# Row maxima kept in six neighbouring columns and transposed once for both heads, with a re-planned order of the work

## The chip, the cores and the metric

The kernel runs as one launch on one core of a Trainium2 chip. The metric is the device time of an execution in microseconds (us). TensorE (PE in the rows) does the matrix products and transpositions, VectorE (DVE) and ScalarE (ACT) read their results out of PSUM, GpSimd (POOL) works from SBUF alone, and SyncE (SP) issues the transfers.

## The reference

Two layers of attention follow each other, for 4 batches of 768 positions, in float32. The first has 8 heads of 64 dimensions; a query attends only to the keys that fall in its own cluster (the nearest of 16 centroids). The second is a mixture of four experts with a causal mask, of which each position uses two:

```python
mask = q_assign[:, :, :, None] == k_assign[:, :, None, :]
scores = scale * np.matmul(q, k.transpose(0, 1, 3, 2))
scores = np.where(mask, scores, -1000000000.0)
scores = scores - np.max(scores, axis=-1, keepdims=True)
attn = np.exp(scores)
attn = attn / (np.sum(attn, axis=-1, keepdims=True) + 1e-09)
...
for e in range(E):
    ...
    scores = np.where(causal, -1000000000.0, scores)
    scores = scores - scores.max(-1, keepdims=True)
    ...
    out += mask[..., None] * w[:, :, kk:kk + 1] * ye
```

What matters here is the row's maximum, which is subtracted before the exponential.

## The kernel before

The work is cut into 24 pairs (`NS`): 16 pairs of heads of the first layer (`n` from 0 to 15), then 8 pairs of experts. A pair holds two heads or experts `h`, and its 768 queries are done in two halves `hf` of 384, each of three chunks `cc` of 128. So there are 48 halves.

For each half, `core(n)` does the same steps:

- **Row matmuls** (L1084): one product per chunk, head and half of the keys gives scores with queries on the partitions, in a PSUM bank of the tag `row` (two banks). VectorE takes the maximum along each row (L1094) into `mx`, and L1099 joins the two key halves into `MT`, a tile of 128 x 2 x 2 x 128 in which chunk `cc` of head `h` and half `hf` has its column at 32 `cc`. The other columns are zero.
- **Transposition of the maxima** (L1106): two TensorE transpositions, one per head, of 128 x 128 from `MT` into one bank of the tag `misc`. The three rows that are wanted come out at partitions 0, 32 and 64.
- **Copy and transfer**: for every pair but the first, ScalarE (L1116) or VectorE (L1119) copies 96 partitions x 256 columns, negated, to `mr`, and two transfers put every 32nd row of `mr` into row `MR` of the query tile `tq`. For the first pair, where the rows start at partitions of 32 each, ScalarE writes them straight into `tq` (L1131, six small copies a half).
- **Scores** (L1158, L1159): two accumulating products per key chunk and head, with keys on the partitions, in a bank of the tag `st` (three banks). The second holds the row `MR`, so that the maximum is subtracted by the product. ScalarE takes the exponential (L1164) into `p` tiles.
- **Values and sums**: products with the values (L1202, two heads beside each other in the array, into the one bank `av`), additions of the `p` tiles on GpSimd (L479) or VectorE (L480), and their sums over keys (L1226).

Before that, `attention_operands(n)` transposes queries and keys (L626), finds each position's cluster, and multiplies the queries by the mask of one half of the clusters: a product of the cluster rows with a block matrix (L766), read by VectorE (L770 for the first pair alone, L776, L782) and ScalarE (`hi`). For the first pair these two products take the banks `row`. In that pair ScalarE also copies cluster rows into `tq` (L734). `moe_operands` does the like for experts with projections (L870, L922). While the first pair waits for its inputs, TensorE runs products with no use (L1330).

The order of the work is written out: each step is an `op` with a number in the order in which it was created, and the table `ORDER` gives for each engine the list of its numbers. `Plan.run` follows that table; each engine executes its list strictly in that order, and a step that may run on two engines runs on the one in whose list it stands. The banks and tiles of a tag are handed out in turn to their users.

Of the kernel before, what the change touches and what calls it, by code (L numbers as in the profile page):

```python
# [10 lines left out]
def _warn_once_fixed(msg, *args, **kwargs):  # L11
# [26 lines left out]
    pe="""  # L38
# [373 lines left out]
def t_mm(n):  # L412

    return max(n / 2400 + 0.015, 0.111)
# [8 lines left out]
def kernel(  # L423
# [133 lines left out]
    for s in range(3):  # L557
        TK.append(consts.tile([128, 2, 2, S], FR, name=f"tk{s}"))
        TQ.append(consts.tile([128, 2, 2, S], FR, name=f"tq{s}"))
    MT = consts.tile([128, 2, 2, 128], FT)  # L560

    def clear_rows(s):
        for h in range(2):
# [821 lines left out]
```

## Time and profile before

| | us |
|---|---|
| median of 3 runs | 722.25 (720.97 to 724.99) |
| profiled execution | 721.82 |
| its span, first to last instruction | 720.1 |
| TensorE busy | 702.6 (98%) |
| VectorE busy | 567.5 (79%) |
| ScalarE busy | 365.8 (51%) |
| GpSimd busy | 303.1 (42%) |

The span is 1.7 us shorter than the time of the same execution; what lies around it is start and end of the launch. "Busy" counts an engine as busy from the start of an instruction to its end. TensorE's matmuls overlap, so two starts that lie 0.18 us apart show as instructions of 0.34 us each: the distance from start to start says what one costs in a stream, not its own duration. In a timeline row, "x2" joins two instructions that follow each other, the second number is the time from the first one's start to the last one's end, and a bracket gives the idle time before it and what ended it.

### The profile page before, as it was taken

The numbers are of one execution on the slowest core, as the hardware profiler recorded it, in microseconds if no ns is written. First come the engines' busy times: TensorE is split into PE (matmuls) and PEld (weight loads), VectorE is DVE, ScalarE is ACT, GpSimd is POOL, SyncE is SP. The second block draws the span as 40 slices with busy tenths as digits, with TensorE's granted clock in tenths as the row PEclk, the third lists the DMA queues.
The fourth block names the chain that finished last, engine by engine and source line by source line (L and its number), as shares of the span: only waits on it lengthen the run. The fifth ranks groups of instructions, "written<-read, shape, count | busy, mean of one in ns | idle before, by whom it ended". The sixth has DMA issues, their size and how long they took to land.

```text
span 720.1 us, 13669 instructions
## 1 busy us (share of the span) xinstructions
PE 702.6 (98%) x4609; PEld 529.2 (73%) x4609; DVE 567.5 (79%) x1279; ACT 365.8 (51%) x904; POOL 303.1 (42%) x245
## 2 busy tenths in 40 slices
PE   6999999999999999999999999999999999999997
PEld 4666767677667677667677688868977987887776
DVE  6989887988888878888889876785598678578844
ACT  4365656556456465456466643464355345333642
POOL 5043467437357575554775632242222223112220
PEclk9999999999999999999999999999999999999999
DMA  7696664685676667595686564445455444455223
GB/s 193 170 195 170 157 173 112 164 221 131 155 201 166 185 166 176 133 232 151 169 213 187 145 175 120 118 126 145 145 130 143 125 123 139 104 125 149 76 77 124
DMA packets 79794, 109.99 MB, mean 153 GB/s; under 512 B 23936, under 2 KB 63212, under 8 KB 79724
## 3 DMA queue, kind: packets, MB, share of 16 engines
q1 hardware_dynamic: 79724, 109.11, 58.5%
q8 instruction: 37, 0.61, 0.4%
q14 instruction: 33, 0.27, 0.1%
HBM read 36.54 MB, written 12.91 MB: 69 GB/s over the span
## 4 chain that ended last, share of the span: by engine, by line
PE 81%; DMA 7%; DVE 4%; SPq 3%; ACT 3%; issue 1%; ACTq 0%; DVEq 0%
PE av L1202 20%; PE row L1084 11%; PE st L1158 11%; PE st L1159 10%; PE misc L870 9%; PE misc L922 5%; PE misc L1315 4%; SPq L467 3%; PE misc L1226 3%; PE misc L626 2%; DVE mx L1094 2%; DMA tq<-hi 2%; PE misc L650 1%; PE misc L1106 1%; DMA tk<-hi 1%
## 5 line engine op out<-in xcount | busy, mean ns | idle before, releaser
L1094 DVE TENSOR_REDUCE mx<-row 128x1 f32<-128x384 f32 (+1 forms) x442 | 232.0, 547 | 49.2 <-PE row L1084 46.0
L1158 PE MATMUL st<-tq,tk 128*128 128x384 f32 (+2 forms) x528 | 182.5, 348 | 2.5 <-ACT p L1164 1.8
L1164 ACT ACTIVATE p<-st 128x384 f32<-128x384 f32 (+2 forms) x304 | 128.5, 459 | 100.4 <-PE st L1159 61.8
L1159 PE MATMUL st<-tq,tk 97*128 97x384 f32 (+2 forms) x528 | 174.0, 332 | 0.4 <-DMA tq<-mr 0.4
L1084 PE MATMUL row<-tk,tq 80*128 80x384 f32 (+3 forms) x506 | 170.0, 359 | 1.7 <-DMA tq<-hi 1.3
L1084 PEld LDWEIGHTS row<-tk,tq 80*128 80x128 f32 (+1 forms) x506 | 92.9, 189 | 28.6 <-DVE mx L1094 9.7
L1158 PEld LDWEIGHTS st<-tq,tk 128*128 128x128 f32 x528 | 100.0, 189 | 16.6 <-issue 6.7
L1159 PEld LDWEIGHTS st<-tq,tk 97*128 97x128 f32 x528 | 100.4, 190 | 1.7 <-DMA tq<-mr 0.7
L479 POOL TENSOR_TENSOR acc<-acc,p 128x768 f32<-128x768 f32 (+2 forms) x39 | 64.8, 1660 | 74.5 <-DVE acc L480 38.0
L479 POOL TENSOR_TENSOR acc<-acc,xl 128x768 f32<-128x768 f32 x29 | 53.2, 1833 | 31.6 <-DVE acc L480 29.0
L474 ACT ACTIVATE hi<-misc 128x384 fp32r<-128x384 f32 x72 | 35.3, 498 | 58.8 <-PE misc L870 37.8
L1164 ACT ACTIVATE xl<-st 128x384 f32<-128x384 f32 x112 | 51.9, 497 | 23.4 <-PE st L1159 22.9
L1164 ACT ACTIVATE xh<-st 128x384 f32<-128x384 f32 x112 | 52.4, 499 | 19.5 <-PE st L1159 18.9
L1169 POOL TENSOR_SCALAR_AFFINE_SELECT p<-p 128x256 f32<-128x256 f32 x48 | 21.3, 457 | 95.6 <-ACT p L1164 70.0
L1202 PE MATMUL av<-p,vt 128*64 128x384 f32 x320 | 59.4, 494 | 0.0
L479 POOL TENSOR_TENSOR acc<-p,p 128x768 f32<-128x768 f32 (+1 forms) x14 | 24.6, 1756 | 72.5 <-ACT p L1164 42.1
L479 POOL TENSOR_TENSOR acc<-acc,xh 128x768 f32<-128x768 f32 x24 | 44.0, 1831 | 22.0 <-DVE acc L480 19.4
L480 DVE TENSOR_TENSOR acc<-acc,p 128x768 f32<-128x768 f32 (+2 forms) x52 | 45.8, 880 | 5.4 <-POOL p L1169 1.7
L1092 DVE TENSOR_TENSOR row<-row,tri 128x128 f32<-128x128 f32 x96 | 28.1, 293 | 19.6 <-PE row L1084 19.4
L1277 POOL TENSOR_TENSOR xt<-avu,rb 128x384 f32<-128x384 f32 x28 | 28.2, 1021 | 35.3 <-DMA rb<-rd 31.3
L1202 PE MATMUL av<-p,vm 128*64 128x384 f32 (+2 forms) x288 | 41.5, 423 | 0.0
L1202 PE MATMUL av<-xl,vt 128*64 128x384 f32 x224 | 40.2, 491 | 0.0
(255 smaller groups left out, 1295.8 us busy)
## 6 DMA issues: line engine op xcount, KB each, us to landing
tq<-hi SPq DMA_DIRECT2D x91, 192.0 KB
tk<-hi SPq DMA_DIRECT2D x60, 192.0 KB
tk<-lo SPq DMA_DIRECT2D x46, 192.0 KB
tq<-lo SPq DMA_DIRECT2D x46, 192.0 KB
rb<-rd SPq DMA_DIRECT2D x46, 192.0 KB
vt<-in_v_dram SPq DMA_DIRECT2D x16, 384.0 KB
x<-xt SPq DMA_DIRECT2D x16, 384.0 KB
tk<-hi SPq DMA_DIRECT2D x16, 384.0 KB
```

What stands on the lines that cost most here:

```text
L474: return op("act", t_act(n, sbuf), lambda: ACT.activation(dst(), src(), AF.Copy), due, after, use, alt=(MO["m_copy"], "dve", t_dve(n), lam ...
L479: ways = [("pool", t_pool(n), lambda: POOL.tensor_tensor(dst(), a(), b(), op=fn)), ("dve", t_dve(n), lambda: DVE.tensor_tensor(dst(), a(), ...
L480: ("dve", t_dve(n), lambda: DVE.tensor_tensor(dst(), a(), b(), op=fn))]
L870: PE.matmul(m()[:, :HW], w_[:, dc, es], x_[dc]()[:, c], start=(i == 0), stop=(i == 3 * DC - 1))
L922: PE.matmul(m()[:, :NV], x_[dc]()[:, ts], w_[:, dc, :], start=(i == 0), stop=(i == 3 * DC - 1))
L1084: PE.matmul(ps()[:, :w], Q[0:R, h, 0, c * 128:(c + 1) * 128], K[0:R, h, 0, i * w:(i + 1) * w], start=True, stop=True)
L1094: DVE.tensor_reduce(to, ps()[:, :w], axis=AX.X, op=OP.max)
L1158: PE.matmul(p()[:, o_:HW], K[:, h, 1, ks], Q[:, h, 1, qs], start=True, stop=False)
L1159: PE.matmul(p()[:, o_:HW], K[0:R, h, 0, ks], Q[0:R, h, 0, qs], start=False, stop=True)
L1164: ACT.activation(pt()[:, h, o_:HW], p()[:, o_:HW], AF.Exp, scale=SC)
L1202: PE.matmul(av()[h * 64:(h + 1) * 64, o_:HW], d["vv"](h, kc), pt()[:, h, o_:HW], start=(kc == 0), stop=(kc == nk - 1), tile_position=(0, 6 ...
L1315: PE.matmul(m(), a_()[:, ts], w_()[:, ep, :], start=(ep == 0 and i == 0), stop=(ep == EP - 1 and i == 2))
```

## The change

1. The maxima of all pairs but the first go into a new tile `M6` of 128 x 2 x 2 x 3: the six columns of a half (two heads, three chunks) lie beside each other. The first pair keeps `MT`.
2. For these pairs one transposition of 128 x 6 gives 6 rows of 128, where two of 128 x 128 gave 128 rows of 256.
3. `mr` shrinks from 96 x 2 x 128 to 6 x 128, and so does its copy; the two transfers read three neighbouring partitions each.
4. The first pair's two mask products (L766) take banks of `st` in place of `row`.
5. The table `ORDER` is another one throughout. 133 steps change between ScalarE and VectorE (69 to VectorE, 64 away), 77 between GpSimd and VectorE (43 to VectorE, 34 away).

```diff
@@ ORDER (a line of each of the five lists; all five are new)
-8 4 15 0 13 1 185 18 189 194 20 196 199 361 23 25 42 201 37 50 58 52 204 68 54 56 70 62 60 206 64 66 72 78 219 80 82
+8 4 15 0 13 1 185 18 189 194 20 196 199 361 23 25 37 42 201 52 50 54 68 66 58 204 64 206 70 60 62 56 78 72 219 82 80
...
+    M6 = consts.tile([128, 2, 2, HC], FT)
...
-            m = misc() if n else plan.buf(psum, "row", (128, 512), FT, 2)
+            m = misc() if n else plan.buf(psum, "st", (128, 512), FT, 3)
...
+            def tops(h, n=n, hf=hf):
+                return M6[:, hf, h] if n else MT[:, hf, h, :32 * HC:32]
...
-                    to = mx()[:, h, cc, i:i + 1] if nb == 2 else MT[:, hf, h, 32 * cc:32 * cc + 1]
+                    to = mx()[:, h, cc, i:i + 1] if nb == 2 else tops(h)[:, cc:cc + 1]
...
-                for h in range(2):
-                    PE.transpose(m()[:, h * 128:(h + 1) * 128], MT[:, hf, h], identf)
+                if n:
+                    PE.transpose(m()[:2 * HC, :128], M6[:, hf].rearrange("p h c -> p (h c)"), identf)
+                else:
+                    for h in range(2):
+                        PE.transpose(m()[:, h * 128:(h + 1) * 128], MT[:, hf, h], identf)
...
-                mr = tmp("mr", (96, 2, 128), FR, bufs=2)
+                mr = tmp("mr", (2 * HC, 128), FR, bufs=2)
...
-                    ACT.activation(mr(), m()[:96, :256].rearrange("p (h j) -> p h j", h=2), AF.Copy, scale=-1.0)
+                    ACT.activation(mr(), m()[:2 * HC, :128], AF.Copy, scale=-1.0)
...
-                        dma(Q[MR:MR + 1, h, 0, hf * HW:(hf + 1) * HW], mr()[0:96:32, h])
+                        dma(Q[MR:MR + 1, h, 0, hf * HW:(hf + 1) * HW], mr()[h * HC:(h + 1) * HC])
```

Three places show how the order moves. The line numbers of the changed kernel are 4 to 7 higher from `core` on (L1088 is the row matmul that was L1084, L1110 the transposition, L1165 and L1166 the scores, L1209 the values, L1233 the sums) and 1 lower in the helpers (L473 and L474 are the copies).

TensorE, pair 7, at the transposition for its second half, which the trace has at 226.0 us; before:

```order
L1226 MATMUL misc_3128<-acc_2816,ones_82 32x192 x4
L1158 MATMUL st_3135<-tq_106,tk_105 128x384
L1159 MATMUL st_3135<-tq_106,tk_105 128x384
L1106 MATMUL misc_3143<-identf,MT 128x128 x2
L1158 MATMUL st_3146<-tq_106,tk_105 128x384
L1159 MATMUL st_3146<-tq_106,tk_105 128x384
L1084 MATMUL row_3151<-tk_107,tq_108 128x384
```

and now:

```order
L1233 MATMUL misc_3120<-acc_2794,ones_82 32x192 x4
L1110 MATMUL misc_3128<-identf,M_110 6x128
L1165 MATMUL st_3130<-tq_106,tk_105 128x384
L1166 MATMUL st_3130<-tq_106,tk_105 128x384
L1088 MATMUL row_3137<-tk_107,tq_108 128x384
L1088 MATMUL row_3140<-tk_107,tq_108 128x384
```

Two transpositions of 128 columns became one of 6, and it moved ahead of one pair of score products, to directly behind the sums.

ScalarE, first pair, from the cluster rows on; before:

```order
L706 ACTIVATE rows_303<-misc_299,row_bias,row_scale 128x384
L474 ACTIVATE hi_335<-row_323 128x384
L474 ACTIVATE hi_335<-row_317 128x384
L734 ACTIVATE tq_104<-rows_303 16x384 x2
L474 ACTIVATE hi_442<-misc_271 128x384
```

and now:

```order
L706 ACTIVATE rows_301<-misc_297,row_bias,row_scale 128x384
L734 ACTIVATE tq_104<-rows_301 16x384 x2
L473 ACTIVATE xk_325<-misc_268 128x384
L473 ACTIVATE hi_344<-st_319 128x384
L473 ACTIVATE hi_344<-st_317 128x384
```

The copies of the cluster rows into `tq` now stand ahead of the masked queries' high parts, and a copy `xk` of the second pair's keys stands between them.

VectorE, first pair, up to the joined maxima of its second half; before:

```order
L1094 TENSOR_REDUCE mx_470<-row_551 128x1
L475 COPY xq_573<-misc_553 128x384
L1094 TENSOR_REDUCE mx_470<-row_579 128x1
L639 TENSOR_TENSOR lo_518<-misc_567,hi_442 128x384
L475 COPY xq_573<-misc_581 128x384
L1094 TENSOR_REDUCE mx_470<-row_599 128x1
L1094 TENSOR_REDUCE mx_470<-row_565 128x1
L1099 TENSOR_REDUCE MT<-mx_470 128x2x3
```

and now:

```order
L1098 TENSOR_REDUCE mx_462<-row_569 128x1
L474 COPY xk_325<-misc_583 128x384
L1098 TENSOR_REDUCE mx_462<-row_590 128x1
L1098 TENSOR_REDUCE mx_462<-row_588 128x1
L1104 TENSOR_REDUCE MT<-mx_462 128x2x3
L639 TENSOR_TENSOR lo_518<-misc_583,hi_480 128x384
```

One of the copies and the subtraction `lo` no longer stand ahead of the joined maxima.

## Rows read from the trace of the kernel before

**Rows 1.** The page's first part: busy us (share of the span) xinstructions.

```profile
PE 702.6 (98%) x4609; PEld 529.2 (73%) x4609; DVE 567.5 (79%) x1279; ACT 365.8 (51%) x904; POOL 303.1 (42%) x245
```

**Rows 2.** Middle stretch: length, busy PE PEld DVE ACT POOL, PEclk, DMA share, GB/s.

```profile
40.00:680.00 640.00, 633.70 (x4163) 478.38 (x4160) 516.59 (x1157) 333.33 (x832) 283.98 (x212) 1.00 0.60 154
```

**Rows 3.** TensorE's timeline around a transposition of 24 columns (start us, us).

```profile
474.71 0.34 PE L1158 MATMUL st<-tq,tk 128*128 128x384 f32 x1
474.88 0.34 PE L1159 MATMUL st<-tq,tk 97*128 97x384 f32 x1
475.06 0.34 PE L1158 MATMUL st<-tq,tk 128*128 128x384 f32 x1
...
475.81 0.33 PE L1159 MATMUL st<-tq,tk 97*128 97x384 f32 x1
475.98 0.27 PE L966 MATMUL misc<-identf,wt 128*24 128x128 f32 x1
476.01 0.42 PE L1084 MATMUL row<-tk,tq 80*128 80x384 f32 x1
476.27 0.34 PE L1158 MATMUL st<-tq,tk 128*128 128x384 f32 x1
```

**Rows 4.** TensorE's timeline around one of the pairs of transpositions.

```profile
225.81 0.34 PE L1159 MATMUL st<-tq,tk 97*128 97x384 f32 x1
225.99 0.38 PE L1106 MATMUL misc<-identf,MT 128*128 128x128 f32 x2
226.13 0.42 PE L1158 MATMUL st<-tq,tk 128*128 128x384 f32 x1
226.39 0.34 PE L1159 MATMUL st<-tq,tk 97*128 97x384 f32 x1
```

**Rows 5.** All transpositions of L1106 and L966: ns min/median/max, first and last start.

```profile
L1106 PEld LDWEIGHTS misc<-identf,MT x96: 137/142/146, 32.3 to 683.1; 128*128 128x128 f32 x96
L1106 PE MATMUL misc<-identf,MT x96: 270/272/332, 32.3 to 683.2; 128*128 128x128 f32 x96
...
L966 PEld LDWEIGHTS misc<-identf,wt x4: 92/93/93, 475.8 to 650.2; 128*24 128x24 f32 x4
```

**Rows 6.** Waits of TensorE's matmuls: us in total, times, longest.

```profile
PE st L1158 <- ACT p L1164: 1.8, 5, 0.6
PE row L1084 <- DMA tq<-hi: 1.3, 3, 0.5
PE misc L1106 <- DVE MT L1099: 1.0, 3, 0.6
...
PE st L1158 <- ACT xh L1164: 0.6, 2, 0.4
PE st L1159 <- DMA tq<-mr: 0.4, 1, 0.4
```

**Rows 7.** Of the waits of TensorE's weight loads, the one for the row banks.

```profile
PEld row L1084 <- DVE mx L1094: 9.7, 22, 0.6
```

**Rows 8.** Copies of the transposed maxima, and a narrower copy, by form: busy, mean ns.

```profile
L1116 ACT ACTIVATE mr<-misc 96x256 fp32r<-96x256 f32 x34 | 12.9, 378 | 27.7 <-PE misc L1106 27.6
L1164 ACT ACTIVATE p<-st 128x128 f32<-128x128 f32 x32 | 8.4, 278 | 5.9 <-PE st L1159 5.8
L1119 DVE TENSOR_SCALAR mr<-misc 96x256 fp32r<-96x256 f32 x12 | 5.0, 414 | 2.5 <-PE misc L1106 2.5
```

**Rows 9.** VectorE's timeline in the first pair, up to its second joined maxima.

```profile
38.30 0.56 DVE L1094 TENSOR_REDUCE mx<-row 128x1 f32<-128x384 f32 x1 [0.90 <-PE row L1084]
39.35 0.56 DVE L639 TENSOR_TENSOR lo<-misc,hi 128x384 fp32r<-128x384 f32 x1 [0.50 <-ACT hi L474]
39.83 0.55 DVE L475 COPY xq<-misc 128x384 f32<-128x384 f32 x1
...
41.34 0.17 DVE L1099 TENSOR_REDUCE MT<-mx 128x6 f32<-128x12 f32 x1
```

More of the change, by code (lines that the diff above doesn't have):

```diff
@@ L1087, in core, with go @@
                 o = op("pe", t_mm(w), go, due, d["half_row"] if early and i == 0 else d["need_row"][hf], used)
-                def go(hf=hf, h=h, cc=cc, i=i, nb=nb, w=w, ps=ps, mx=mx):
+                def go(h=h, cc=cc, i=i, nb=nb, w=w, ps=ps, mx=mx, tops=tops):
                     if moe and i == nb - 1:
@@ L1097, in core, with go @@
             if two:
-                def go(hf=hf, mx=mx, two=two):
-                    DVE.tensor_reduce(MT[:, hf, :, 32 * two[0]:128:32][:, :, :len(two)], mx()[:, :, two[0]:], axis=AX.X,
-                                      op=OP.max)
+                def go(n=n, hf=hf, mx=mx, two=two):
+                    to = M6[:, hf, :, two[0]:] if n else MT[:, hf, :, :32 * HC:32]
+                    DVE.tensor_reduce(to, mx()[:, :, two[0]:], axis=AX.X, op=OP.max)
                 maxes.append(op("dve", 0.13, go, due + 0.6, maxes + last, [mx]))
             m = misc()
-            def go(hf=hf, m=m):
-                for h in range(2):
-                    PE.transpose(m()[:, h * 128:(h + 1) * 128], MT[:, hf, h], identf)
+            def go(n=n, hf=hf, m=m):
+                if n:
[3 more added lines that the diff above has]
+                        PE.transpose(m()[:, h * 128:(h + 1) * 128], MT[:, hf, h], identf)
             due = t_r + DUE["top"] + 6 * DUE["row_step"] * hf
-            o = op("pe", 2 * t_mm(128), go, due, maxes, [m])
+            o = op("pe", t_mm(128) if n else 2 * t_mm(128), go, due, maxes, [m])
             d["m_pe"].append(o)
@@ L1111, in core @@
             if n:
-                mr = tmp("mr", (96, 2, 128), FR, bufs=2)
+                mr = tmp("mr", (2 * HC, 128), FR, bufs=2)
                 def go_a(m=m, mr=mr):
-                    ACT.activation(mr(), m()[:96, :256].rearrange("p (h j) -> p h j", h=2), AF.Copy, scale=-1.0)
+                    ACT.activation(mr(), m()[:2 * HC, :128], AF.Copy, scale=-1.0)
                 def go_d(m=m, mr=mr):
-                    DVE.tensor_scalar(mr(), m()[:96, :256].rearrange("p (h j) -> p h j", h=2), -1.0, None, op0=OP.mult)
-                o = op("act", t_act(256), go_a, due + 0.4, [o], [m, mr], alt=(MO["m_copy"], "dve", t_dve(256), go_d))
+                    DVE.tensor_scalar(mr(), m()[:2 * HC, :128], -1.0, None, op0=OP.mult)
+                o = op("act", t_act(128), go_a, due + 0.4, [o], [m, mr], alt=(MO["m_copy"], "dve", t_dve(128), go_d))
                 def go(hf=hf, mr=mr):
                     for h in range(2):
-                        dma(Q[MR:MR + 1, h, 0, hf * HW:(hf + 1) * HW], mr()[0:96:32, h])
+                        dma(Q[MR:MR + 1, h, 0, hf * HW:(hf + 1) * HW], mr()[h * HC:(h + 1) * HC])
                 outs.append(op("sp", 2 * [(0.78, 0.05)], go, due + 0.5, [o] + sets_free(n), [mr]))
```

331 rows, old and new, of tables (act, dve, pe, pool) are left out of this document.

## The prediction

> **What bounds the kernel now.** I read three views in turn. The page's first part gives TensorE 98% busy, VectorE 79%, ScalarE 51%, GpSimd 42% [rows 1]. A busy share alone does not say that an engine sets the time, so the second view is the busy time of the middle, from 40 to 680 us: TensorE is idle there for 640 - 633.70 = 6.3 us in all, at the full granted clock (1.00, the level of 2.4 GHz) [rows 2]. The third is the timeline, since TensorE's instructions overlap: three score products of 384 columns start at 474.71, 474.88 and 475.06, 0.175 us apart while each shows 0.34 us [rows 3]. So TensorE issues products back to back, each held up only by the one ahead of it. What it no longer has to issue in the middle comes off the end, unless a wait swallows it.
>
> The Trainium skill speaks against the first of these readings (Trainium Kernel Development and Optimization, Performance Expectations): matmul busy time is a poor measure because matmuls are pipelined, and the share of the weight loads is a better one. By that, 529.2 us or 73% [rows 1] leaves a quarter of the span open. The trace agrees that the busy share overstates the work, and settles it by the spacing of the starts, which leaves no gap in the rows shown. The forecast goes by the spacing.
>
> **The change part by part.**
>
> Transpositions. There are 96 of L1106 [rows 5]; 4 are the first pair's and stay, so 92 in 46 steps become 46. What a pair costs in the stream: from the L1159 at 225.81 to the L1159 at 226.39 lie 0.58 us, in which TensorE starts a product, the two transpositions and another product [rows 4]. Two products without anything between take 475.06 - 474.71 = 0.35 us [rows 3], so the pair costs 0.23. What a single narrow one costs is in the trace too: L966 transposes 24 columns to 24 rows. From the L1159 ahead of it at 475.81 to the L1158 behind the next product at 476.27 lie 0.46 us; less 0.35 that is 0.11 [rows 3]. The difference is 0.12 by these rounded starts; half of the pair is 0.115, and I take 0.115. 46 x 0.115 = 5.3 us less on TensorE.
>
> The load of 24 columns shows 93 ns against 142 for 128 [rows 5], yet its transposition costs in the stream what half a pair costs. A rule of the Trainium skill would give more (TensorE: Matmul & The Clock Gate, LDWEIGHTS): a weight load takes its columns divided by 1.2 GHz, so 6 columns load some 100 ns sooner than 128. If that set the transposition's place in the stream, the sum would be lower by an estimated 46 x 0.10 = 4.6 us. The trace does not bear it out, neither in the load's duration nor in its cost; it stands among the rivals with a price from rows.
>
> Copies of the maxima. 34 on ScalarE at 378 ns and 12 on VectorE at 414 [rows 8] read 128 columns in place of 256. A ScalarE row with 128 columns has 278 ns, so I take 0.10 us less each, 4.6 us over both engines. It lies beside TensorE's work: ScalarE is busy for 51%. It also brings `tq` forward by 0.1 us per half, but only one wait of TensorE was for that transfer, 0.4 us [rows 6]. I count nothing; the bounds are 0 and -0.4.
>
> Transfers. The same two per half, with the same bytes into `tq`; only the source's partitions lie closer. Nothing.
>
> Joined maxima in `M6`. The same reductions with the same inputs, written to neighbouring columns in place of columns 32 apart. No row shows whether that pitch costs a write anything. VectorE's instruction at the joined maxima of the first pair is 0.17 us long with the wide pitch [rows 9], which bounds a gain by 46 x 0.17 on an engine with slack; a loss has no reason, since the new columns are contiguous. Nothing.
>
> First pair. ScalarE's copies into `tq` move ahead of the high parts, and the row products find their two banks free of the mask products, so these products can start earlier. But until the first joined maxima VectorE has the same list of instructions to do in the old and the new order, and it is the engine that is busy there. Only behind that does something move: a subtraction and a copy no longer stand ahead of the second joined maxima. The subtraction took 0.56 us, behind 0.50 of waiting for ScalarE [rows 9]; the copy's place is taken by another one. So the second joined maxima may come up to 1.1 us sooner, and TensorE, which by then also has the second pair's operands to work on, gains between nothing and that: I take -0.4. On the other side, the first row products that use `st` banks must now wait for a subtraction L782 on VectorE; the nearest row is VectorE's wait of 0.90 for a row product there [rows 9], so the other bound is +0.9.
>
> The new order elsewhere. TensorE's list moves its steps by two places on average and holds the same work. In the place shown the transposition comes two products sooner after the maxima, 0.35 us less time for VectorE to finish; elsewhere it comes later. 14 steps more end up on VectorE, at some 0.5 to 0.95 us each about 10 us on an engine that is idle for 150. I cost the order at nothing on balance, and this is the largest unknown: the prices are in the rivals.
>
> What waits swallow. Where TensorE waits for something that does not move with it, the time saved since the last such wait is lost. In the middle it waited 3 + 3 + 5 + 2 + 1 = 14 times for VectorE, ScalarE or a transfer, for 5.1 us [rows 6]. Most releasers (exponentials of scores, maxima of row products) themselves follow TensorE's work and come earlier with it; the transfers do so less. Half of 14 waits, each swallowing one step's 0.115, is 0.8 us. The bounds are 0 and all 14, 1.6 us.
>
> The sum, made against the profiled execution: 721.82 - 5.3 - 0.4 + 0.8 = 716.9 us. That execution lies 0.43 under the median of the runs, so I predict 717.3 us. What a measurement of this kernel can tell from no change is about 0.5%, or 3.6 us; faster means below 718.6, slower above 725.9.
>
> **The rivals.**
>
> The new order waits more for the row banks (slower). The place is the row product, L1084, whose weights wait for VectorE's maximum of the product two before it: 9.7 us in 22 waits, 0.44 each, in the old order [rows 7]. They lie inside TensorE's busy time, so its 98% would hide more of them. VectorE gets 14 steps more, and each that stands between two maxima can add such a wait. To end over 725.9 the order must add 725.9 - 717.3 = 8.6 us, 20 waits, nearly twice what there was; at 24 more the time is 728. For it: all five lists are new, and VectorE has the most work after TensorE. Against it: VectorE is idle for a fifth of the span [rows 1], and over 48 halves only 22 such waits stood. Chance 0.12.
>
> The saving is swallowed (no change). The 0.115 us of a step is small beside the waits, and if the transfers' chain rather than TensorE sets the pace of a pair, what TensorE saves it waits for later. It decides from 718.6 - 717.3 = 1.3 us on, three more waits of 0.44 at the row banks; with half of the 5.3 us gone the time is 720 us. For it: VectorE must finish a pair's maxima, 24 of them, and its other work within each pair. Against it: 6.3 us of idle time in 640 [rows 2]. It is also how the change would fail to do what it says. Chance 0.22.
>
> The narrow weight load shortens the remaining transposition as well. If what is loaded sets the transposition's place in the stream, one of 6 columns costs next to nothing in place of 0.11, and the sum falls by up to 46 x 0.11 = 5.1 us more, to 712.2. For it: the load of 24 columns is shorter than that of 128 [rows 5]. Against it: the one of 24 columns in the rows still cost the full 0.11 [rows 3]. This is the page's rule on weight loads taken to its end. Chance 0.06.
>
> **How the numbers follow.** The forecast, TensorE bound and the saving passed on, has 0.60, with its own range from 715.0 (no wait swallows anything, the first pair gains 0.9 and the order gives 1) to 719.5 (all 14 waits swallow and the order costs 1.4). About 0.06 of it lies above 718.6. Faster: 0.54 + 0.06 from the weight load + 0.03 of the swallowed case = 0.63. Slower: 0.12. Within 0.5%: 0.25. The range that should hold the time 8 times in 10 goes from 713.0, which leaves out the fullest gain of the narrow load, to 724.0, which takes in the swallowed case and a worse order up to 15 more waits at the row banks, and leaves out the slower one.
>
> **What would show it.** Right: the spacing around the single transposition is 0.46 for two products and it, as with L966; 50 transpositions of L1110 and L1113 in place of 96; TensorE's idle time in the middle still near 6 us; the waits of row products for maxima still near 10 us. First pair: the second joined maxima some 0.4 us earlier than 41.34. Wrong: the transposition costs 0.2 us although it is one; or the waits of L1088's weights for maxima go well above 22; or the middle's idle time rises by as much as the transpositions saved, at the transfers of `tq` and `tk`.

## The result, and the profile after

| | before | changed |
|---|---|---|
| median of the runs (us) | 722.95 (720.97 to 724.99) | 714.91 (714.00 to 716.05) |
| profiled execution (us) | 721.82 | 715.09 |
| its span (us) | 720.1 | 713.4 |
| granted clock of TensorE | 0.999 | 0.999 |

The ratio is 0.989, interval 0.986 to 0.992: faster by 1.1%. Two other comparisons gave 0.986 (0.983 to 0.989) and 0.985 (0.982 to 0.988). The gain is 8 to 11 us. The kernel before has four runs here, one more than at the time of the prediction. Forecast were 717.3 us with a range from 713.0 to 724.0: the sign came out, and so did the mechanism of the largest term, the transpositions. The gain was larger than the 4.9 us of the sum (5.3 + 0.4 - 0.8).

The first part of the page, which answers to [rows 1], shows each engine's busy time, its share of the span and its instructions:

```profile
PE 696.5 (98%) x4562; PEld 521.5 (73%) x4562; DVE 568.3 (80%) x1293; ACT 363.0 (51%) x899; POOL 295.1 (41%) x236
```

TensorE has 47 instructions less (46 transpositions, and a record more or less) and is busy 6.1 us less; VectorE has the 14 steps more that the new order gives it, and is busy 0.8 us longer. The span fell by 6.7. The middle stretch, in the form of [rows 2] but cut at 673 us since the span is shorter (length, busy time of PE, PEld, DVE, ACT and POOL, granted clock, DMA share, GB/s):

```profile
40.00:673.00 633.00, 626.75 (x4110) 470.11 (x4107) 518.45 (x1171) 328.37 (x821) 278.14 (x204) 1.00 0.60 156
```

TensorE is idle there for 633.00 - 626.75 = 6.25 us, against 6.3 before [rows 2]. It is bound as it was. What it doesn't have to issue came off the end.

The transpositions, all of one line, with the durations in ns (least, median, most) and the first and last start; they answer to [rows 5]:

```profile
L1110 PEld LDWEIGHTS misc<-identf,M x46: 82/85/88, 55.9 to 675.9; 128*6 128x6 f32 x46
L1110 PE MATMUL misc<-identf,M x46: 271/272/275, 56.0 to 676.1; 128*6 128x128 f32 x46
L1113 PE MATMUL misc<-identf,MT x4: 272/300/328, 31.4 to 41.3; 128*128 128x128 f32 x4
```

46 and 4 in place of 96. Each still shows 272 ns, and that isn't its cost, since it lies beside its neighbours. The cost stands in the starts around it, read here from TensorE's timeline (start, duration, line, tiles), which answers to [rows 4]:

```profile
206.29 0.34 PE L1166 MATMUL st<-tq,tk 97*128 97x384 f32 x1
206.47 0.27 PE L1110 MATMUL misc<-identf,M 128*6 128x128 f32 x1
206.49 0.42 PE L1088 MATMUL row<-tk,tq 80*128 80x384 f32 x1
206.75 0.38 PE L662 MATMUL misc<-identf,s 128*128 128x128 f32 x2
```

From the L1166 at 206.29 to the L662 at 206.75 lie 0.46 us for two products and the transposition, where two products alone take 0.35 [rows 3]. It costs 0.11, as did the one of 24 columns.

What TensorE waited for, in the form of [rows 6] (us in total, times, longest):

```profile
PE st L1165 <- ACT p L1171: 2.1, 4, 0.7
PE row L1088 <- DMA tq<-hi: 1.2, 3, 0.8
PE st L1165 <- ACT xh L1171: 1.1, 2, 0.7
PE misc L1110 <- DVE M L1104: 0.6, 1, 0.6
...
PE st L1088 <- DVE lo L782: 0.4, 1, 0.4
```

and of its weight loads, the row that answers to [rows 7]:

```profile
PEld row L1088 <- DVE mx L1098: 12.5, 29, 0.6
```

The matmuls' waits are about what they were. The wait for the row banks has grown from 9.7 us in 22 to 12.5 in 29, and yet the kernel is faster: one of the places where the prediction's signs have to be read with care.

### The profile page after: what moved, and what is told of

Its sections match the earlier page's. It is cut to its first block, busy times and chain, and to the rows that moved or that the text cites. A ratio compares the mean times of both kernels' runs of the same rounds, so it can differ in the third digit from the quotient of the medians.

```text
span 713.4 us, 13574 instructions
## 1 busy us (share of the span) xinstructions
PE 696.5 (98%) x4562; PEld 521.5 (73%) x4562; DVE 568.3 (80%) x1293; ACT 363.0 (51%) x899; POOL 295.1 (41%) x236
## 4 chain that ended last, share of the span: by engine, by line
PE 80%; DVE 6%; DMA 5%; SPq 4%; ACT 3%; issue 1%; ACTq 0%; DVEq 0%
PE av L1209 19%; PE st L1165 11%; PE row L1088 11%; PE st L1166 10%; PE misc L870 9%; PE misc L922 5%; SPq L466 4%; PE misc L1322 4%; PE misc L1233 3%; PE misc L626 2%; DMA tq<-hi 2%; DVE mx L1098 2%; DMA kt<-in_k_dram 2%; PE misc L650 1%; DMA vm<-x 1%
## 5 line engine op out<-in xcount | busy, mean ns | idle before, releaser
L1165 PE MATMUL st<-tq,tk 128*128 128x384 f32 (+2 forms) x528 | 182.6, 348 | 3.2 <-ACT p L1171 2.1
L1171 ACT ACTIVATE p<-st 128x384 f32<-128x384 f32 (+2 forms) x304 | 130.0, 458 | 109.6 <-PE st L1166 68.2
L1166 PE MATMUL st<-tq,tk 97*128 97x384 f32 (+2 forms) x528 | 173.7, 332 | 0.0
L1088 PE MATMUL row<-tk,tq 80*128 80x384 f32 (+4 forms) x506 | 168.0, 359 | 1.7 <-DMA tq<-hi 1.2
L1165 PEld LDWEIGHTS st<-tq,tk 128*128 128x128 f32 x528 | 99.9, 189 | 21.4 <-issue 7.0
L1088 PEld LDWEIGHTS row<-tk,tq 80*128 80x128 f32 (+1 forms) x506 | 93.2, 189 | 27.3 <-DVE mx L1098 12.5
L1166 PEld LDWEIGHTS st<-tq,tk 97*128 97x128 f32 x528 | 100.3, 190 | 0.8
L478 POOL TENSOR_TENSOR acc<-acc,p 128x768 f32<-128x768 f32 (+2 forms) x34 | 58.6, 1723 | 85.8 <-DVE acc L479 52.7
L473 ACT ACTIVATE hi<-misc 128x384 fp32r<-128x384 f32 x71 | 34.7, 493 | 54.6 <-PE misc L870 34.3
L1209 PE MATMUL av<-p,vt 128*64 128x384 f32 x320 | 60.0, 494 | 0.9 <-ACT p L1171 0.6
L478 POOL TENSOR_TENSOR acc<-acc,xh 128x768 f32<-128x768 f32 x28 | 51.4, 1839 | 21.9 <-DVE acc L479 8.1
L478 POOL TENSOR_TENSOR acc<-acc,xl 128x768 f32<-128x768 f32 x27 | 49.5, 1833 | 18.0 <-DVE acc L479 9.3
L1284 POOL TENSOR_TENSOR xt<-avu,rb 128x384 f32<-128x384 f32 x24 | 24.2, 1016 | 45.3 <-DMA rb<-rd 38.5
L1209 PE MATMUL av<-p,vm 128*64 128x384 f32 (+2 forms) x288 | 41.5, 423 | 0.0
L1209 PEld LDWEIGHTS av<-p,vt 128*64 128x64 f32 x320 | 21.0, 136 | 26.8 <-issue 23.9
L1209 PE MATMUL av<-xl,vt 128*64 128x384 f32 x224 | 40.2, 491 | 0.0
L1209 PE MATMUL av<-xh,vt 128*64 128x384 f32 x224 | 39.9, 490 | 0.0
```

What stands on the lines that cost most here:

```text
L473: return op("act", t_act(n, sbuf), lambda: ACT.activation(dst(), src(), AF.Copy), due, after, use, alt=(MO["m_copy"], "dve", t_dve(n), lam ...
L478: ways = [("pool", t_pool(n), lambda: POOL.tensor_tensor(dst(), a(), b(), op=fn)), ("dve", t_dve(n), lambda: DVE.tensor_tensor(dst(), a(), ...
L1088: PE.matmul(ps()[:, :w], Q[0:R, h, 0, c * 128:(c + 1) * 128], K[0:R, h, 0, i * w:(i + 1) * w], start=True, stop=True)
L1165: PE.matmul(p()[:, o_:HW], K[:, h, 1, ks], Q[:, h, 1, qs], start=True, stop=False)
L1166: PE.matmul(p()[:, o_:HW], K[0:R, h, 0, ks], Q[0:R, h, 0, qs], start=False, stop=True)
L1171: ACT.activation(pt()[:, h, o_:HW], p()[:, o_:HW], AF.Exp, scale=SC)
```

## The experiments

Nine kernels made twelve runs, in three groups of four, each group on one chip beside the kernel before; the first two groups share a chip. A table or a sentence names the median of the kernel before, by which a group is known (724.22, 723.83 and 725.43). Each ratio is to the kernel before beside it, with its 95% interval. It is not the quotient of the two medians, so a gain taken from it can differ from theirs by about 1 us.

### The old transposition in the new order, and the new one in the old order

Of the edits, two can stand alone: how the maxima are transposed, and the order (with the banks of the first pair). The first kernel has the new order and the new banks, with the transpositions and copies of before:

```diff
-                if n:
-                    PE.transpose(m()[:2 * HC, :128], M6[:, hf].rearrange("p h c -> p (h c)"), identf)
-                else:
-                    for h in range(2):
-                        PE.transpose(m()[:, h * 128:(h + 1) * 128], MT[:, hf, h], identf)
+                for h in range(2):
+                    PE.transpose(m()[:, h * 128:(h + 1) * 128], MT[:, hf, h], identf)
...
-                mr = tmp("mr", (2 * HC, 128), FR, bufs=2)
+                mr = tmp("mr", (96, 2, 128), FR, bufs=2)
```

> The new order and the new banks, with the old transposition put back: MT with wide columns, two transpositions of 128 columns per half, copies of 96 x 256. If TensorE's stream sets the time, 46 more transpositions at 0.112 us cost 5.2 us: 714.9 + 5.2 = 720.1 us, from 719 to 721. If the gain is the order's and the transpositions lie beside waits, the time stays at 715 to 716.

The second is the kernel before with these lines the other way round (the new transposition), in the old order and with the old banks.

> The old order and the old banks, with the new transposition alone (six neighbouring columns, one transposition, the narrow copy). TensorE's stream: 722.95 - 5.2 = 717.8 us, from 717 to 719. Order alone: no change, 722 to 723. The difference between this and the new kernel, some 2.8 us, is then what the new order and the banks bring.

The third has all edits of the code, the banks too, in the old order:

> All edits of the code with the old order, so the new kernel less its order. TensorE's stream: as with the new transposition alone, 717.8 us, with 0.4 either way for the banks of the first pair. If the new order brings what the prediction missed, this stays 2 to 3 us above the new kernel; if the missing 2.4 us are the transposition's (shorter copies, fewer weight columns), it lies at 715 like the new kernel.

| kernel | us (median) | ratio to before (724.22) |
|---|---|---|
| new order, old transposition | 720.58 | 0.9964 (0.9943 to 0.9984) |
| old order, new transposition | 720.41 | 0.9945 (0.9926 to 0.9964) |
| old order, all code edits | 720.26 | 0.9955 (0.9934 to 0.9975) |

Each half gains by itself: the transposition 0.55% or 4.0 us, the order with its banks 0.36% or 2.6 us (interval 1.2 to 4.1). I had costed the order at nothing beyond the 0.4 us of the first pair. The first expectation came out. The other two missed: both kernels were to take 717.8 us, some 5.2 under the kernel before, and lay only 3.8 and 4.0 under it by their medians. So the old order stands more than 5 us above the new kernel (714.67 on this chip in the next group), and not 2 to 3. Because these are differences near the noise, both were run again beside the new kernel on another chip, with no edit beyond those above:

> The new kernel, on one chip with both single edits: 0.986 to 0.989 of the kernel before, as in its two measurements so far.

> The new order and banks with the old transposition, beside the new kernel on one chip. If the two edits simply add up, the transposition is worth the same here as in the old order, some 4 to 5 us, and this lies at 0.993 to 0.995. If the new order only pays together with the new transposition, for which it was laid out, this lies at 0.996 to 1.0, 7 us over the new kernel.

> The new transposition alone in the old order and banks, on the same chip: 0.9945 again. With what the old transposition in the new order gives, the two shares are to add up to the new kernel's within 1.5 us if they are independent; over 2.5 us missing would be the part that needs both.

| kernel | us (median) | ratio to before (725.43) |
|---|---|---|
| new kernel | 715.08 | 0.9850 (0.9823 to 0.9878) |
| new order, old transposition | 720.79 | 0.9949 (0.9921 to 0.9976) |
| old order, new transposition | 720.17 | 0.9915 (0.9886 to 0.9944) |

Here the transposition alone is worth 0.85% or 6.2 us and the order alone 0.51% or 3.7 us. Their sum, 1.36%, is what the new kernel gains, 1.50%, within the intervals. So in this group the two parts add. On the other chip it is less clear: there the two single gains make 0.91%, 6.6 us, and the new kernel, in another group, gained 1.40%, 10.1 us. Whether up to 3.5 us need both parts together stays open. On top of the new transposition the order is worth more than alone: 720.17 - 715.08 = 5.1 us here.

The mean of the two comparisons is 5.1 us for the transposition alone (forecast 5.3) and 3.1 us for the order alone (forecast 0.4, for the first pair).

In both kernels the waits for the row banks are already near those of the new one. The weight loads' row of the new order with the old transposition, and then of the old order with the new one:

```profile
PEld row L1083 <- DVE mx L1093: 12.6, 29, 0.7
```

```profile
PEld row L1089 <- DVE mx L1099: 12.0, 29, 0.6
```

So the seven more waits don't belong to the new order alone: they also come in the old one with the new transposition. Part of the seven lies within what other traces of the old order show: the kernel before with the edit of the banks alone has 26 (10.8 us). In the old order with the new transposition a wait that grows because TensorE has less to issue between two maxima would fit; that is argued and not shown.

### The banks of the first pair alone

The kernel before with one edit, so that part 4 of the change stands alone:

```diff
-            m = misc() if n else plan.buf(psum, "row", (128, 512), FT, 2)
+            m = misc() if n else plan.buf(psum, "st", (128, 512), FT, 3)
```

> The kernel before with the first pair's two mask products in the banks of the scores, nothing else. VectorE's list, which this leaves alone, sets the first pair, so the prediction's -0.4 for the first pair must come from the order: 1.000, within 0.002. If the row banks held the first products up: 0.4 to 0.9 us faster, at the edge of what the runs can tell; if the scores' banks are held too long: slower by as much.

724.80 us against 725.43, ratio 0.9989 (0.9966 to 1.0013): nothing that can be measured. By the middle value, 0.8 us, most of the 3 us above belongs to the order; the interval leaves up to 0.34%, 2.5 us, to the banks. They don't show in the first table either, where the old order with the new transposition takes 720.26 us with them and 720.41 without.

### The narrow transposition more than once

Does a transposition cost by its number, or by its columns? The new kernel issues each narrow one twice, so that there are again 92, of 6 columns each (the copies of the maxima stay narrow):

```diff
-                    PE.transpose(m()[:2 * HC, :128], M6[:, hf].rearrange("p h c -> p (h c)"), identf)
+                    for _ in range(2):
+                        PE.transpose(m()[:2 * HC, :128], M6[:, hf].rearrange("p h c -> p (h c)"), identf)
```

> The new kernel with its narrow transposition issued twice in all 46 halves; copies, transfers and order stay. TensorE's stream, where a transposition costs its place and not its columns: 46 x 0.112 = 5.2 us more, 720.1 us, as with the old transposition. If the shorter copies and the sooner row of maxima carried the gain: 715.0 to 715.5. If a load of six columns makes a transposition nearly free: under 716.

720.10 us against 724.22, ratio 0.9943 (0.9921 to 0.9965). On the same chip the new order with two wide transpositions took 720.58. So two narrow ones cost what two wide ones cost: the medians differ by 0.5 us, with intervals of some 1.5 us either way. Nor does the smaller copy of the maxima, narrow in the one and wide in the other, give more than that. Against the new kernel on this chip, in the next group, 46 more narrow ones cost 720.10 - 714.67 = 5.4 us: the full price.

The same four times, beside the new kernel on one chip:

```diff
+                    for _ in range(4):
```

> The new kernel with the narrow transposition issued four times in all 46 halves: 138 more. If each takes its 0.112 us of the stream, 15.5 us over the new kernel on the same chip. If a part is hidden beside waits, less: at 0.09 each (what twice against the first measurement of the new kernel suggests across chips) 12.4 us. If the new kernel's gain hung on shorter copies, 1 us.

> The new kernel once more, on the chip of the three that follow, so that they can be set beside it: 0.989 of the kernel before. If the first measurement of the new kernel was a low draw, 0.992, which is the sum of the two single edits (0.9945 and 0.9964 give 0.991).

725.09 us against 714.67; the ratios to before (723.83) are 1.0013 (0.9998 to 1.0028) and 0.9860 (0.9832 to 0.9888). TensorE's timeline of the kernel with four:

```profile
208.00 0.34 PE L1167 MATMUL st<-tq,tk 97*128 97x384 f32 x1
208.18 0.60 PE L1111 MATMUL misc<-identf,M 128*6 128x128 f32 x4
208.54 0.42 PE L1088 MATMUL row<-tk,tq 80*128 80x384 f32 x1
208.80 0.38 PE L662 MATMUL misc<-identf,s 128*128 128x128 f32 x2
```

From the score product to the L662 it is 0.80 us, where it was 0.46 with one: 0.34 for three more, 0.113 each, the same as the first. In the stream 138 more cost 138 x 0.113 = 15.6 us. At the end they cost 725.09 - 714.67 = 10.4, less than the 12.4 of the expectation. A third was swallowed, by the medians all of it behind the first 46. Part of where shows in the middle stretch of this kernel, in the columns of the windows above:

```profile
40.00:673.00 633.00, 629.55 (x4183) 475.83 (x4181) 512.00 (x1153) 324.17 (x811) 274.22 (x201) 1.00 0.60 154
```

TensorE is idle there for 3.45 us in place of 6.25. The other 2.4 us of the swallowed 5.2 I can't place: the waits for the row banks, inside its busy time, are the same 29. Swallowing is real in this kernel, when work is added.

### The 210 steps that change engine

The new order does two things: other sequences, and 210 steps on other engines. The next kernel keeps the new sequences and puts the 210 steps back on the engine of before, each at its place in time in that engine's list. TensorE's list and SyncE's stay as they are; a stretch of VectorE's, with an ellipsis on either side, shows two steps that come back:

```diff
@@ ORDER (210 steps put back in the lists of VectorE, ScalarE and GpSimd)
-... 87 89 216 93 91 95 218 101 358 97 99 ...
+... 87 89 216 93 91 367 95 218 101 369 97 99 ...
```

> The new kernel, with each of the 210 steps that moved between VectorE, ScalarE and GpSimd put back on its old engine, at the place in time that the new order gave it; the other steps keep the new order. If the part of the gain that the transposition does not explain comes from the new shares of the engines: 2.5 us slower than the new kernel. If it comes from the order on TensorE: the same as the new kernel, within 1 us. Steps put back may also collide at their new neighbours: up to 5 us slower, which would tell nothing of the shares.

And the old order, with all code edits, in which the 210 steps go to their new engine:

> All edits of the code with the old order, and the 210 moved steps put on the engines that the new order gives them. If the shares of the engines bring the rest: 2.5 us faster than the old order with the same code (0.9955), so 0.992. If the order on TensorE brings it: no faster than 0.9955, and slower where the moved steps collide.

729.72 us against 723.83, ratio 1.0073 (1.0054 to 1.0092), and 737.09, ratio 1.0184 (1.0153 to 1.0214). Parted in this way each half costs: 15 us (against the new kernel's 714.67) and 17 us (against the 720.26 of the old order with all code edits, in another group). The first expectation allowed for 5 us at most, the second named no figure. From 40 to 673 us TensorE is busy for 618.10 us in the first and 615.13 in the second, so idle for 14.9 and 17.9. The weight loads' waits for the row banks, first and second:

```profile
PEld row L1089 <- DVE mx L1099: 16.2, 40, 0.9
```

```profile
PEld row L1088 <- DVE mx L1098: 19.6, 41, 1.3
```

This is near what the slower rival describes: 40 waits at the row banks. But these are the smaller part. In the first kernel they are 16.2 - 12.5 = 3.7 us longer than in the new one, and TensorE's idle time in the middle is 14.9 - 6.25 = 8.65 longer, of 15 us in all. And the two kernels mix what they test with a placement that nobody planned, so they don't tell whether the 3 us of the new order come from the sequences or from the engines. They show only that this way of parting them costs more than the order brings.

## Why the prediction was right, and where its size was off

**TensorE's spacing sets the time: right.** The middle's idle time stayed at 6.25 us, and 138 transpositions more made the kernel slower, while a smaller copy on ScalarE and VectorE moved nothing that shows. The busy share alone would have said the same, but it would have priced a transposition at its 0.27 us. The Trainium skill's warning that matmul busy time is a poor measure (Trainium Kernel Development and Optimization, Performance Expectations) agrees with the trace on that point. The share of the weight loads, which the Trainium skill names there among the good measures of how close a kernel is to the limit, is 73% before and after; the trace shows that this share didn't tell whether the change would pay.

**Transpositions, -5.3 us: right, mechanism and size.** 0.11 us each in the stream; -4.0 and -6.2 us measured alone, and 720.79 - 715.08 = 5.7 us on top of the new order.

**The narrow load (the rival at 712.2 us): wrong.** The load of 6 columns shows 85 ns, that of 24 columns 93, that of 128 columns 142 [rows 5]: narrower is shorter, but not in proportion, and none of it shows in the starts. By the Trainium skill's rule (TensorE: Matmul & The Clock Gate, LDWEIGHTS), columns divided by 1.2 GHz, 6 columns would load in an estimated 5 ns. The trace differs, and it decides. At 714.9 us the kernel lies about as near this rival's 712.2 as the forecast's 717.3, so the total alone could not have told them apart; the kernels that repeat the narrow transposition do.

**Copies of the maxima, nothing: right.** They fell by more than the 0.10 us taken (378 to 260 and 414 to 272 ns), and at the end it is worth nothing that can be measured. The new rows, which answer to [rows 8] (busy us, mean ns, idle before):

```profile
L1123 ACT ACTIVATE mr<-misc 6x128 fp32r<-6x128 f32 x29 | 7.5, 260 | 24.1 <-PE misc L1110 23.2 <-DMA tk<-hi 0.5
L1126 DVE TENSOR_SCALAR mr<-misc 6x128 fp32r<-6x128 f32 x17 | 4.6, 272 | 3.4 <-PE misc L1110 3.1
```

**First pair, -0.4 us: within its bounds, for another reason.** VectorE's timeline, which answers to [rows 9], has the second joined maxima at 39.80 in place of 41.34. That is 1.5 us sooner, more than the 1.1 given as its bound. The prediction had it that VectorE does the same list up to the first joined maxima, is the busy engine there, and that only behind them something moves. In the traces the first joined maxima themselves come 0.95 us sooner. VectorE waits ahead of them for TensorE's products L685, and that wait is 1 us shorter (0.4 us in the seven traces of the new order, 1.0 to 1.8 in the five of the old). The list is two copies shorter as well, which brought nothing: just ahead of the wait VectorE starts L676 at 14.29 in place of 14.19. Before:

```profile
16.21 0.55 DVE L695 SCALAR_TENSOR_TENSOR oh<-misc,oh 128x48 bf16<-128x48 f32 x4 [1.46 <-PE misc L685]
32.13 0.16 DVE L1099 TENSOR_REDUCE MT<-mx 128x6 f32<-128x12 f32 x1
```

and now:

```profile
15.26 0.55 DVE L695 SCALAR_TENSOR_TENSOR oh<-misc,oh 128x48 bf16<-128x48 f32 x4 [0.41 <-PE misc L685]
31.18 0.16 DVE L1104 TENSOR_REDUCE MT<-mx 128x6 f32<-128x12 f32 x1
39.80 0.17 DVE L1104 TENSOR_REDUCE MT<-mx 128x6 f32<-128x12 f32 x1
```

TensorE's first value product starts 0.5 us sooner, at 38.88 in place of 39.40. Over all traces it starts at 39.4 to 40.3 in the five kernels with the whole old order and at 38.4 to 39.2 in the seven with the whole new one, so the gain is real, 0.95 us between the means; that it lies near the -0.4 taken is luck. The wait that the banks of `st` bring is there too, at 0.4 us of the 0.9 allowed; TensorE's timeline with the idle time before an instruction in brackets:

```profile
22.37 0.44 PE L1088 MATMUL st<-tk,tq 128*128 128x384 f32 x1 [0.37 <-DVE lo L782]
```

**The new order elsewhere, nothing on balance: this is the step that was mis-sized.** It was named as the largest unknown. Order, banks and first pair together were worth -3.1 us alone, as the mean of -2.6 and -3.7, where the sum has -0.4. With -3.1 in its place the 717.3 becomes 714.6, against 714.9 measured. The 14 steps more on VectorE, put at about 10 us, raised its busy time by 0.8, since other steps left it. Where the gain came from is only in part found. The same value products in both profiled executions, by their starts on TensorE:

| value product at (before to after, us) | gain | narrow transpositions by then | at 0.113 each | rest |
|---|---|---|---|---|
| 39.40 to 38.88 | 0.5 | 0 | 0 | 0.5 |
| 116.67 to 114.21 | 2.5 | 5 | 0.6 | 1.9 |
| 344.61 to 339.53 | 5.1 | 23 | 2.6 | 2.5 |
| 554.65 to 548.38 | 6.3 | 37 | 4.2 | 2.1 |
| 702.80 to 696.04 | 6.8 | 46 | 5.2 | 1.6 |

In these two executions the rest seems to be there by 117 us. The other traces don't bear that out. At that product TensorE has nine instructions fewer behind it in the new order, the transpositions counted alike; they come later. In the second trace of the new kernel the gain is 2.8 us there, and at the product that starts at 168.66 before it is -0.1, behind a wait of 2.3 us for a transfer of `tq`; at the last product it is 6.4. At the last product the kernel before and the one with the banks alone, which share the old order, differ by 3.7 us. So single traces don't place a gain of 3 us.

What does repeat is one wait of TensorE, for the clusters of a pair at 105 us; before:

```profile
PE misc L685 <- DVE oh L676: 0.8, 1, 0.8
```

It stands at 0.8 us in all five traces of the old order, and is gone or at most 0.4 in the seven of the new. With the 0.5 to 0.95 us of the first pair that is 1.3 to 1.75 of the 3.1. Which steps bring the remainder stays open, and the two kernels meant to part the sequences from the engines could not tell.

**What waits swallow, +0.8 us: not told apart.** The 14 waits of [rows 6] were taken as waits of the middle, but the rows are of the whole execution; from 40 to 680 us the waits for the exponentials `p` are 3 and not 5, and the one for `oh` above was left out. That makes 13 and changes the term by under 0.1 us. The transposition alone gave 5.1 of its 5.3 us on average, which leaves 0.2 swallowed, with an uncertainty of more than the 0.8. Added work was swallowed by a third. For work that is taken away no run shows that much.

**The order waits more at the row banks (the slower rival, 728 us): its sign came, its price did not.** The waits went from 22 to 29, which the prediction had listed as a sign that it was wrong. They are 28 to 30 in every kernel with either half of the change, each faster than before. With 40 and 41 of them, and more idle time on top, the kernels were indeed slower, though the longer waits make up only 3.7 of the first one's 15 us. The planned order didn't set that off.

**The saving is swallowed (720 us): fell.** All comparisons of the new kernel exclude 720.

## What to carry to other kernels

Where TensorE issues products without a gap, price an instruction by what it adds between the starts of its neighbours, not by its duration: here 0.11 us for a transposition that shows 0.27, and the same for weights of 6 columns as of 128. Merging two such transpositions pays by their number; making the weights of one narrower does not. All of them had 128 moving columns; what fewer would cost no run here shows. When a change comes with a new hand-set order, give that order a term of its own with a bound on either side, and run order and edit apart before saying which of them made the gain.

## What of the hardware was not expected

The cost of an fp32 transposition of 128 moving columns in a full stream didn't depend on the width of its weights: 0.11 us for 6 and for 24 columns, and 0.115 for 128, while the load itself went from 85 over 93 to 142 ns. Repeating it is linear: two products with none, one, and four of them between take 0.35, 0.46 and 0.80 us. The three loads lie on a line of 82 ns plus 0.47 ns per column, an estimate from these widths alone: most of a narrow load is the part that doesn't shrink with the columns. The loads of other products rise faster from nearly the same start: 110 ns for 32 columns (L650), 137 for 64 (L1209) and 190 for 128 (L1166), an estimated 84 ns plus 0.83 ns per column.
